# An attention and expert kernel on one core: band tables loaded by SyncE ahead of most value loads, all key tails of the first two batches copied by VectorE, and an instruction order planned with new landing times

## The chip, the core and the metric

The kernel runs on one core of one Trainium2 chip. The metric is the device time of one execution in microseconds (us). A time below is the median of the executions of a kernel, with the number of executions or the range. Profiled executions have a span, which is the profiler's own measure of the same execution and lies 1.7 to 2.4 us below the device time.

Engines are called TensorE (PE in the profile; PEld is its weight load), VectorE (DVE), ScalarE (ACT), GpSimd (POOL) and SyncE (SP, which here only issues DMAs). A ratio is the mean time of one kernel's fast runs over the mean time of the fast runs of the kernel before in the same rounds on the same chip, so it is not quite the ratio of the medians quoted beside it.

## The reference

The reference is attention with a relative position bias, followed by one expert layer with a sine gate. All inputs and the output are float32.

```python
# attention: q, k, v are (8 batches, 8 heads, 576, 64), bias_table is (32, 8)
scores = matmul(q, k^T) / sqrt(64) + bias_table[bucket(|i - j|)]   # bucket is constant for far keys
attn   = exp(scores - max); attn = attn / (sum(attn) + 1e-9)
x      = matmul(attn, v)            # heads put side by side: (8*576, 512) = (4608, 512)
# expert: w_in (512, 2048), w_out (2048, 512), alpha (2048,)
h = x @ w_in
g = h + sin(alpha * h)**2 / (alpha + 1e-9)
out = g @ w_out                     # (4608, 512)
```

The bias of far keys is one constant per head, so only a band near the diagonal needs correcting. The kernel multiplies that band of exp(scores) by exp(bias difference).

## The kernel before

The kernel works batch by batch, two heads (a "pair", `p`) at a time. Score matmuls go into a PSUM tile `sc`; ScalarE writes exp(sc) into a buffer `u`; VectorE multiplies the near-diagonal band of `u` by tables `m2r` and `mhr`; TensorE multiplies `u` by the values (`v`, and `vh` for the last 64 keys); the result is normalized and transposed into `xT`; the expert matmuls `sc<-xT,w_in`, the sine, the square, `g` and the `w_out` matmuls follow. The expert stage of one batch is mixed with the attention of later ones.

Three details matter.

First, the band tables are made on the chip: a small matmul and exp give an 8-row table `e_sb`, which is written to DRAM (`e_dram`, 8 KB) and read back with overlapping rows as `m2r` and `mhr`. These reads must wait for the write.

Second, the last 64 keys of a pair are multiplied from a block-diagonal copy `kts` (`kt` in the profile, the "key tails"). In the kernel before, VectorE makes that copy for pairs 0 and 1 of the first batch, and small DMAs of SyncE make it for all others.

Third, everything after the prologue is ordered by a greedy list scheduler, written in Python and run when the kernel is built. It knows only assumed durations and assumed landing times of the loads. Each engine then executes its instructions in that fixed order, whatever really happens.

```python
T_M2 = (16.8, 20.0)        # m2r: first two heads, rest
T_MH = (18.0, 18.0)        # mhr
T_V = (18.5, 45.0)         # values of batch 0, of batch 1
T_TR1 = (33.0, 37.0)       # keys and queries of batch 1
T_W = 30.0                 # w_in
T_WO = (48.5, 50.5, 52.5, 54.0)
FAR = 1
...
class Plan:
    def run(self, t0):
        free = {e: t0 for e in ("PE", "ACT", "DVE", "POOL", "DMA", "SP")}
        todo = list(self.tasks)
        while todo:                      # pick the task that may start first, by the
            ...                          # assumed times; emit it; advance that engine
```

The prologue, cut to what the change touches (`P_` is GpSimd):

```python
    nc.sync.dma_start(out=id_sb, in_=idm.ap())
    ...
    for c in range(4):                                   # values of batch 0: 6 loads, SyncE
        nc.sync.dma_start(out=vst[0][:, c], in_=vp[128 * c : 128 * c + 128])
    for z in range(2):
        nc.sync.dma_start(out=vhst[0][64 * z : 64 * z + 64], in_=vq[z, 512:S])
    ...
    nc.scalar.activation(out=e_sb, in_=eps_[0:H, 0:EW], func=AF.Copy)
    nc.scalar.dma_start(out=e_dram.ap(), in_=e_sb)       # 8 KB write
    cast0(0, nc.vector)
    cast0(1, P_)
    clear(P_, 1)
    load_m2r(P_, 0, 2)                                   # reads of e_dram, by GpSimd
    load_mhr(P_)
    cast_v(0, P_, (0, 1))                                # values to 16 bit
    load_m2r(P_, 2, H)
    load_w_in16((0,))
    cast_v(0, P_, (2, 3, 4, 5))
    load_w_in16((1, 2, 3))
    for kq, src in ((0, k), (1, q)):
        load_nat(nat2[:, kq], 0, H, src[1], P_)          # keys, queries of batch 1
    load_v32(1, P_)
    load_w_out16()
    cast_v(1, P_, range(6))
```

The key tails:

```python
        far = kq == 0 and (t == 1 or p > FAR)
        ...
        if far:                          # by a DMA of SyncE, for one or two pairs at a time
            ...
            def split(e):
                load_kt(t, p0, p1)
            y = plan.add({"DMA": D_SPLIT}, split, [z[1] for z in ps_], pri)
            ...
            return [x], []

        def tail(e):                     # by VectorE
            for z in range(2):
                r = slice(64 * z, 64 * z + 64)
                nc.vector.tensor_copy(
                    out=kts[t][r, p, r], in_=kTs[t][r, p, 512:S]
                )
```

The softmax here doesn't subtract the row's maximum and nothing guards it: scores larger than these inputs give would overflow.

Of the kernel before, what the change touches and what calls it, by code (L numbers as in the profile page):

```python
# [24 lines left out]
def t_act(n):  # L25
    return n / 1200.0 + 0.052
# [27 lines left out]
class Cell:  # L54
    v = None
# [123 lines left out]
T_MODE = 0.11  # L179
T_START = 7.0  # L180
T_PAIR = ((7.0, 8.5), (10.5, 13.0), (10.5, 13.0))
T_M2 = (16.8, 20.0)
T_MH = (18.0, 18.0)
T_V = (18.5, 45.0)
T_TR1 = (33.0, 37.0)
D_SPLIT = 3.5
T_W = 30.0
# [1 line left out]
WARM0 = 6  # L189
WARM1 = 1  # L190
AV_PRI = 2000
FAR = 1
NORM_PRI = -300
CP_PRI = -1
SIN_SET = "trig_and_small"
# [15 lines left out]
def kernel(  # L211
# [11 lines left out]
    nc = tc.nc  # L223
    T, H, S, D = q.shape
# [48 lines left out]
    vst, vhst = [], []  # L273
# [108 lines left out]
    def load_kt(t, p0, p1):  # L382
        for z in range(2):
            r = slice(64 * z, 64 * z + 64)
            nc.sync.dma_start(out=kts[t % 2][r, p0:p1, r], in_=kTs[t % 2][r, p0:p1, 512:S])
# [16 lines left out]
                out=vhs[t % 2][64 * z : 64 * z + 64, :, VC * z : VC * z + D], in_=vq[z, 512:S]  # L402
            )

    def load_v32(t, eng):
        vp = v[t].rearrange("h s d -> s h d")
        for c in range(4):
            eng.dma_start(out=vst[t][:, c], in_=vp[128 * c : 128 * c + 128])
        vq = v[t].rearrange("(hp two) s d -> two s hp d", two=2)
        for z in range(2):  # L410
            eng.dma_start(out=vhst[t][64 * z : 64 * z + 64], in_=vq[z, 512:S])

    def cast_v(t, eng, cs):
        for c in cs:
            if c < 4:
                eng.tensor_copy(out=vs[t][:, c, :, 0:D], in_=vst[t][:, c])
                continue
            z = c - 4
            eng.tensor_copy(
                out=vhs[t][64 * z : 64 * z + 64, :, VC * z : VC * z + D],  # L420
                in_=vhst[t][64 * z : 64 * z + 64],
            )

    def load_nat(dst, h0, h1, src, eng):

        eng.dma_start(out=dst, in_=src[h0:h1].rearrange("h (p i) d -> p h (i d)", i=SI))
# [35 lines left out]
    def load_m2r(eng, h0, h1):  # L462

        eng.dma_start(
            out=m2r[:, h0:h1],
            in_=bass.AP(tensor=e_dram, offset=EW * h0, ap=[[1, 128], [EW, h1 - h0], [1, XW]]),
        )

    def load_mhr(eng):
        for z in range(2):  # L470
            eng.dma_start(  # L471
                out=mhr[64 * z : 64 * z + 64],
                in_=bass.AP(tensor=e_dram, offset=EW * z + 192,
                            ap=[[1, 64], [2 * EW, NP], [1, 192]]),
            )

    P_ = nc.gpsimd
# [4 lines left out]
        out=tabL,  # L482
        in_=bass.AP(tensor=bias_table.tensor, offset=bias_table.offset + (NB - 1) * H,
                    ap=[[0, NB], [1, H]]),
# [2 lines left out]
    nc.scalar.dma_start(out=alphaN, in_=moe_alpha.rearrange("(f p) -> f p", p=128))  # L487
    nc.scalar.dma_start(out=idf_sb, in_=idf.ap())
    nc.sync.dma_start(out=id_sb, in_=idm.ap())
    nc.scalar.preload_act_table_set(EXP_SET)  # L490
    for kq, src in ((0, k), (1, q)):
        load_nat(nat1[:, kq, 0:2], 2, 4, src[0], P_)
    vp = v[0].rearrange("h s d -> s h d")
    for c in range(4):
        nc.sync.dma_start(out=vst[0][:, c], in_=vp[128 * c : 128 * c + 128])
    vq = v[0].rearrange("(hp two) s d -> two s hp d", two=2)
    for z in range(2):
        nc.sync.dma_start(out=vhst[0][64 * z : 64 * z + 64], in_=vq[z, 512:S])
    for kq, src in ((0, k), (1, q)):
        load_nat(nat1[:, kq, 2:6], 4, H, src[0], P_)  # L500

# [10 lines left out]
    cast0(0, nc.vector)  # L512
    cast0(1, P_)
    clear(P_, 1)
    load_m2r(P_, 0, 2)
    load_mhr(P_)
    cast_v(0, P_, (0, 1))
    load_m2r(P_, 2, H)
    load_w_in16((0,))
    cast_v(0, P_, (2, 3, 4, 5))  # L520
    load_w_in16((1, 2, 3))
    for kq, src in ((0, k), (1, q)):
        load_nat(nat2[:, kq], 0, H, src[1], P_)
# [4 lines left out]
    plan = Plan()  # L528
# [8 lines left out]
        else:  # L537
            k_of(e).tensor_copy(out=o, in_=i)  # L538

    farq, split_of = [], {}  # L540

    def plan_tr(t, p, kq, pri, nb, deps=()):

        b, c = Buf("moE"), Cell()
        far = kq == 0 and (t == 1 or p > FAR)

        def mm(e):
            c.v = bank("moE").bitcast(F16)
            for i in range(SI):
                x = i * SN  # L550
                if t == 0 and p == 0:
                    nc.tensor.transpose(
                        out=c.v[:, x : x + SN], in_=natb[:, kq, i], identity=id_sb[0:SN, 0:SN]
                    )
                    continue
                for z in range(2):
                    h = 2 * p - 2 + z if t == 0 else 2 * p + z
                    nc.tensor.transpose(
                        out=c.v[64 * z : 64 * z + 64, x : x + SN],
                        in_=(nat1 if t == 0 else nat2)[:, kq, h, D * i : D * i + D],  # L560
                        identity=id_sb[0:SN, 0:SN],
                    )

        def cp(e):
            pin = c.v[:, 0:S].rearrange("d (i p) -> d p i", i=SI)

            dst = (qTs if kq else kTs)[t][:, p, :]
            copy_on(e, dst.rearrange("d (p i) -> d p i", i=SI), pin)

        m = plan.add({"PE": 0.4 if t == 0 and p == 0 else 0.5}, mm, deps, pri, nb, new=[b])  # L570
        eng = {"DVE": 0.75, "ACT": 0.72}
        if t == 0:
            eng = {"ACT": 0.72} if p == 0 and kq else {"DVE": eng["DVE"]}
        x = plan.add(eng, cp, [m], pri, use=[b])
        if kq:
            return [x], [x]
        if far:
            farq.append((p, x))
            if t and p % 2 == 0:
                return [x], []  # L580
            ps_ = [y for y in farq]
            farq.clear()
            p0, p1 = ps_[0][0], ps_[-1][0] + 1

            def split(e):
                load_kt(t, p0, p1)

            y = plan.add({"DMA": D_SPLIT}, split, [z[1] for z in ps_], pri)
            for z in ps_:
                split_of[(t, z[0])] = y  # L590
            return [x], []

        def tail(e):
            for z in range(2):
                r = slice(64 * z, 64 * z + 64)
                nc.vector.tensor_copy(
                    out=kts[t][r, p, r], in_=kTs[t][r, p, 512:S]
                )

        return [x], [plan.add({"DVE": 0.25}, tail, [x], pri + 30)]  # L600
# [90 lines left out]
    def plan_ex(t, y, sc, b, u, ub, m, gate, base, done):  # L691

        p, i = y

        def ex(e):
            uz = u.v[:, 0:8, :].rearrange("p (z c) q -> p z c q", z=2)
            if i == "t":
                o = u.v[:, 8, :].rearrange("p (b q) -> p b q", b=2)
                x = sc.v[:, :, 0:288]
            elif i < 4:  # L700
                o, x = uz[:, :, i, 0:512], sc.v
            else:
                o = uz[:, :, :, 512:576]
                x = sc.v[:, :, 0:256].rearrange("p z (c q) -> p z c q", c=4)
            nc.scalar.activation(out=o, in_=x, func=AF.Exp, scale=0.125)  # L705

        n = 576 if i == "t" else 1024 if i < 4 else 512
        x = plan.add({"ACT": t_act(n)}, ex, [m] + gate, base + 20, use=b + [ub])
        if i == "t":

            def bh(e):
                io = u.v[:, 8, 384:576]
                nc.vector.tensor_tensor(out=io, in0=io, in1=mh[:, p, 0:192], op=ALU.mult)

            done[(0, 4)] = x
            done[(1, 4)] = plan.add({"DVE": 0.19}, bh, [x], base + 10,
                                     nb=0.0 if t else T_MH[p > 0], use=[ub])
            return x
        w = 0 if i < 4 else 1
        q0, n = QW[w]  # L720
        for cc in [i] if i < 4 else range(4):
            done[(w, cc)] = x
            lo, hi = max(q0, 128 * cc - 128), min(q0 + n, 128 * cc + 256)
            if lo >= hi:
                continue

            def bd(e, cc=cc, lo=lo, hi=hi):
                io = u.v[:, 0:8, lo:hi].rearrange("p (z c) q -> p z c q", z=2)[:, :, cc]
                x0 = lo - 128 * cc + 128
                nc.vector.tensor_tensor(  # L730
                    out=io, in0=io, in1=m2[:, 2 * p : 2 * p + 2, x0 : x0 + hi - lo],
                    op=ALU.mult,
                )

            done[(w, cc)] = plan.add({"DVE": 0.1 + (hi - lo) / 960.0}, bd, [x], base + 10,
                                     nb=0.0 if t else T_M2[p > 0], use=[ub])
        return x

# [3 lines left out]
    def plan_av(t, p, w, u, ub, done):  # L742
# [14 lines left out]
        for i, qc in enumerate(QC[w]):  # L757

            def mm(e, i=i, qc=qc):
# [5 lines left out]
                for z in range(2):  # L765
                    for c in range(4):
# [4 lines left out]
            prev = [plan.add({"PE": 0.31}, mm, us + prev, base + AV_PRI + i,  # L771
                             nb=T_V[t] if t < 2 else 0.0, new=[ab] if i == 0 else [],
                             use=[ub] if i == 0 else [ub, ab])]
# [266 lines left out]
```

## Time and profile before

| kernel before | |
|---|---|
| time | 392.61 us, median of 3 runs (392.54 to 392.93) |
| span of the profiled execution | 392.2 us |
| TensorE busy | 96% |
| first value matmul of batch 0 | 19.60 us |
| first expert matmul | 35.80 us |
| first score matmul of the third batch | 54.96 us |

The last three are marks from the timeline: the first ends the load phase, the second ends the start, and the third ends the first expert stage. After them comes a steady stretch of some 337 us.

The first fence shows the head of the page of the kernel before: the span, the busy time of each engine with its share and number of instructions, and three of the rows that cut the span into 40 slices of 9.8 us each. In these rows a digit is the busy share in tenths (PE, DMA), or the granted clock of TensorE in tenths (PEclk).

```profile
span 392.2 us, 8566 instructions
...
PE 378.4 (96%) x3401; PEld 190.1 (48%) x3401; DVE 262.0 (67%) x587; ACT 323.9 (83%) x458; POOL 81.9 (21%) x96
...
PE   6989999999999999999999999999999999999995
...
PEclk9989999999999999999999999999999999999999
DMA  9999999999726999991996497211014000020122
```

TensorE is full except in the first slices and the last, and the DMA row reads 9 in each of the first ten slices, 98 us.

The next fence shows the kernel before in four stretches cut at the marks. The columns are start and end, length, busy time of TensorE, its weight load, VectorE, ScalarE and GpSimd with their instructions, then granted clock, DMA share and GB/s. (The DMA share adds up the times of packets over 16 engines; it exceeds 1 here, up to 1.44.)

```profile
0.00:20.00 20.00, 16.16 (x135) 7.24 (x135) 9.84 (x25) 12.12 (x15) 13.00 (x28) 1.00 1.03 191
20.00:36.00 16.00, 13.62 (x234) 9.82 (x233) 12.47 (x44) 12.06 (x15) 8.25 (x12) 0.89 1.13 205
36.00:55.00 19.00, 17.47 (x167) 8.70 (x165) 15.43 (x29) 16.30 (x29) 14.59 (x17) 1.00 1.44 205
55.00:392.00 337.00, 331.18 (x2872) 164.31 (x2871) 224.24 (x492) 283.41 (x401) 46.09 (x40) 1.00 0.83 92
```

The last stretch has TensorE busy for 331 of 337 us. So a change of the first 55 us moves the total one for one, as long as the steady stretch stays as it is.

The chain of waits of the kernel before (start, duration, what) shows how the tables come in:

```profile
7.04 5.33 DMA e_dram<-e_sb
...
12.66 0.73 POOL m2r L464
13.39 1.27 POOL mhr L471 x2
14.66 1.08 POOL v L416 x2
15.74 6.42 DMA m2r<-e_dram
```

The 8 KB write takes 5.33 us; GpSimd then issues the reads with value casts in between, so that the larger part of `m2r` is issued only at 15.74 us and lands at 22.16 us.

Lines of the timeline of the kernel before, in order of time (start, duration, engine, line, operation, in brackets the idle time before and what ended it):

```profile
17.89 0.61 PE L450 MATMUL sc<-qT,kT 64*128 64x512 f16 x2
...
17.94 2.35 DVE L730 TENSOR_TENSOR u<-u,m2r 128x512 f16<-128x512 f16 x4 [2.24 <-DMA m2r<-e_dram]
...
18.24 1.31 POOL L419 CAST vh<-w_out 64x256 f16<-64x256 f32 x2
...
19.60 0.22 PE L450 MATMUL am<-vh,u 128*128 128x130 f16 x1
...
22.18 0.42 DVE L730 TENSOR_TENSOR u<-u,m2r 128x512 f16<-128x512 f16 x1 [1.43 <-DMA m2r<-e_dram]
...
35.80 0.81 PE L450 MATMUL sc<-xT,w_in 128*128 128x512 f16 x3
...
54.96 0.39 PE L450 MATMUL sc<-qT,kT 64*128 64x512 f16 x2 [0.64 <-DVE g L879]
```

VectorE stands idle for 3.7 us in all for the two parts of `m2r`. The last value cast ends at 19.55 us, and the first value matmul starts 0.05 us later. (The value casts read from `w_out`, because the space of `w_out` holds the raw values at the start.)

A warning about the clock: the profile counts full clock until the first change that it recorded, which is at 19.3 us in the kernel before. The matmuls show that this is wrong: the two score matmuls at 17.89 us took 0.61 us and two of the same form at 54.96 us took 0.39 us, so TensorE was not at full clock there, although PEclk reads 9.

### The profile page before, as it was taken

To read this page: it belongs to the slowest core of one execution; us is meant where nothing else is said; L and a number is where in the kernel's file an instruction comes from. 1 tells how busy PE (TensorE), PEld (TensorE's weight loads), DVE (VectorE), ACT (ScalarE), POOL (GpSimd) and SP (SyncE) were. 2 spreads that over 40 slices of the span, in tenths; PEclk is the share of its full clock that TensorE was granted. 3 is DMA by queue.
4 is the path that set the end of the run, shared out by engine and by line. 5 is a ranking of instruction groups with operands and counts; after the bars stand their busy time and mean duration, and the time that the engine had idled before them with its cause. 6 is when DMAs were issued, how large, how long until landed. Compare 5 with 4: busy or idle time off the path is not lost.

```text
span 392.2 us, 8566 instructions
## 1 busy us (share of the span) xinstructions
PE 378.4 (96%) x3401; PEld 190.1 (48%) x3401; DVE 262.0 (67%) x587; ACT 323.9 (83%) x458; POOL 81.9 (21%) x96
## 2 busy tenths in 40 slices
PE   6989999999999999999999999999999999999995
PEld 2456445644455554445445544554445444444442
DVE  3576987768576689567967895768676869429100
ACT  2976999979899999999989999999999969539211
POOL 5762963090004545001700310000000000000000
PEclk9989999999999999999999999999999999999999
DMA  9999999999726999991996497211014000020122
GB/s 170 211 204 219 207 171 158 166 171 148 92 59 83 158 155 157 158 166 47 150 170 101 34 93 166 68 33 42 27 43 59 17 28 29 27 80 2 57 76 80
DMA packets 148647, 41.99 MB, mean 107 GB/s; under 512 B 137784, under 2 KB 142992, under 8 KB 148608
## 3 DMA queue, kind: packets, MB, share of 16 engines
q0 software_dynamic: 89872, 19.04, 56.9%
q1 hardware_dynamic: 58512, 22.36, 30.3%
q8 instruction: 26, 0.43, 0.5%
q14 instruction: 13, 0.11, 0.1%
q10 hardware_dynamic: 224, 0.05, 0.1%
HBM read 37.76 MB, written 16.52 MB: 138 GB/s over the span
## 4 chain that ended last, share of the span: by engine, by line
PE 86%; DMA 4%; DVE 4%; ACT 3%; POOL 1%; issue 1%; ACTq 0%; DVEq 0%
PE sc L450 41%; PE am L450 34%; PE cb L450 5%; PE ca L450 5%; ACT u L705 2%; DMA m2r<-e_dram 2%; DMA e_dram<-e_sb 1%; DMA phi_sb<-phi_const 1%; DVE g L879 1%; DVE u L730 1%; ACT s L865 1%; DVE xn L785 1%; DVE outs L538 0%; DVE kT L538 0%; POOL mhr L471 0%
## 5 line engine op out<-in xcount | busy, mean ns | idle before, releaser
L705 ACT ACTIVATE u<-sc 128x1024 f16<-128x1024 f32 (+1 forms) x192 | 157.8, 898 | 14.4 <-PE sc L450 12.9
L450 PE MATMUL sc<-xT,w_in 128*128 128x512 f16 x576 | 132.3, 379 | 0.6 <-DVE g L879 0.5
L879 DVE SCALAR_TENSOR_TENSOR g<-sq,inv_a,sc 128x512 f16<-128x512 f16 x144 | 103.3, 746 | 22.1 <-PE am L450 14.7
L450 PE MATMUL am<-w_out,g 128*128 128x512 f16 x416 | 108.6, 380 | 0.3 <-DVE outs L538 0.2
L865 ACT ACTIVATE s<-sc,alphaT 128x512 f16<-128x512 f32 x144 | 92.7, 678 | 6.4 <-PE sc L450 5.0
L730 DVE TENSOR_TENSOR u<-u,m2r 128x512 f16<-128x512 f16 (+2 forms) x160 | 67.7, 438 | 32.4 <-ACT u L705 27.8
L450 PEld LDWEIGHTS <-w_in 128*128 128x128 f16 x576 | 55.3, 98 | 65.0 <-issue 1.3
L450 PEld LDWEIGHTS <-g 128*128 128x128 f16 x576 | 53.3, 98 | 64.1 <-issue 11.6
L450 PEld LDWEIGHTS <-u 128*128 128x128 f16 x1440 | 55.8, 98 | 19.2 <-issue 11.0
L450 PE MATMUL sc<-qT,kT 64*128 64x64 f16 (+1 forms) x512 | 50.8, 297 | 1.7 <-ACT u L705 0.9
L450 PE MATMUL am<-v,u 128*128 128x65 f16 x1152 | 51.2, 194 | 0.0
L872 ACT ACTIVATE sq<-s 128x512 f16<-128x512 f16 x79 | 49.2, 628 | 2.2 <-DVE g L879 0.5
L396 POOL DMA_DIRECT2D v<-in_v_dram x24 | 22.2, 1065 | 119.6 <-PE am L450 104.3
L874 DVE TENSOR_TENSOR sq<-s 128x512 f16<-128x512 f16 x65 | 27.4, 423 | 9.2 <-ACT s L865 8.8
L450 PE MATMUL am<-vh,u 128*128 128x130 f16 x144 | 32.2, 224 | 0.8 <-DVE xp L785 0.8
L450 PEld LDWEIGHTS <-kT 64*128 64x128 f16 x512 | 14.7, 96 | 28.5 <-issue 24.3
L785 DVE TENSOR_TENSOR xp<-am,rd 128x384 f16<-128x384 f32 (+1 forms) x48 | 23.6, 491 | 1.8
L784 DVE RECIPROCAL rd<-am 128x6 f32<-128x6 f32 (+1 forms) x56 | 10.5, 187 | 19.7 <-PE am L450 19.2
L450 PE MATMUL cb<-w_out,g 128*128 128x512 f16 x96 | 23.0, 380 | 0.0
L937 ACT ACT_TABLE_LOAD x13 | 16.7, 1283 | 0.2
L377 POOL DMA_DIRECT2D staged_q<-in_q_dram x6 | 15.5, 2583 | 3.6 <-DMA staged_q<-in_q_dram 3.6
L538 DVE COPY outs<-am 128x512 f32<-128x512 f32 x19 | 13.1, 688 | 4.3 <-PE am L450 4.1
(88 smaller groups left out, 175.6 us busy)
## 6 DMA issues: line engine op xcount, KB each, us to landing
out_dram<-outs SPq DMA_DIRECT2D x36, 256.0 KB, 2.2
staged_k<-in_k_dram POOLq DMA_DIRECT2D x6, 576.0 KB, 13.8
staged_q<-in_q_dram POOLq DMA_DIRECT2D x6, 576.0 KB, 19.7
v<-in_v_dram POOLq DMA_DIRECT2D x24, 128.0 KB, 7.0
w_in<-in_moe_w_in_dram POOLq DMA_DIRECT2D x4, 512.0 KB, 8.8
w_out<-in_moe_w_out_dram POOLq DMA_DIRECT2D x4, 512.0 KB, 10.7
w_out<-in_v_dram SPq DMA_DIRECT2D x4, 256.0 KB, 8.2
v1st<-in_v_dram POOLq DMA_DIRECT2D x4, 256.0 KB, 16.6
```

The lines of the kernel that those rows point to most:

```text
L377: nc.gpsimd.dma_start(out=dst.ap()[t].rearrange("s (h d) -> s h d", h=H), in_=src[t].rearrange("h s d -> s h d"),)
L396: nc.gpsimd.dma_start(out=vs[t % 2][:, c, :, 0:D], in_=vp[128 * c : 128 * c + 128],)
L450: nc.tensor.matmul(out=out, lhsT=lhsT, rhs=rhs, start=start, stop=stop)
L538: k_of(e).tensor_copy(out=o, in_=i)
L705: nc.scalar.activation(out=o, in_=x, func=AF.Exp, scale=0.125)
L730: nc.vector.tensor_tensor(out=io, in0=io, in1=m2[:, 2 * p : 2 * p + 2, x0 : x0 + hi - lo], op=ALU.mult,)
L785: nc.vector.tensor_tensor(out=y.rearrange("p c (z d) -> p c z d", z=2), in0=a[:, :, :, 0:D], in1=r.unsqueeze(3).to_broadcast([128, nq, 2, ...
L865: nc.scalar.activation(out=s16.v, in_=h.v, func=AF.Sin, scale=alphaT[:, f : f + 1])
L872: nc.scalar.activation(out=sq.v, in_=s16.v, func=AF.Square)
L874: k_of(e).tensor_tensor(out=sq.v, in0=s16.v, in1=s16.v, op=ALU.mult)
L879: nc.vector.scalar_tensor_tensor(out=gcell[b].v[:, f, :], in0=sq.v, scalar=inv_a[:, f : f + 1], in1=h.v, op0=ALU.mult, op1=ALU.add,)
L937: nc.scalar.preload_act_table_set(name)
```

## The change

The change wants the tables earlier. It lets SyncE issue their reads, and puts four of the six value loads behind them. It makes all key tails of the first two batches by VectorE copies instead of DMAs. And it plans the order with landing times that are thought to fit the new loads.

```diff
-T_M2 = (16.8, 20.0)
-T_MH = (18.0, 18.0)
-T_V = (18.5, 45.0)
+T_M2 = (13.0, 15.5)
+T_MH = (14.0, 14.0)
+T_V = (18.0, 45.0)
...
-FAR = 1
... (load_v32 takes the chunks to load as an argument: cs=range(6))
     nc.sync.dma_start(out=id_sb, in_=idm.ap())
+    load_v32(0, nc.sync, range(2))
...
-    (four loads vst[0], two loads vhst[0], all on nc.sync)
...
-    load_m2r(P_, 0, 2)
-    load_mhr(P_)
-    cast_v(0, P_, (0, 1))
-    load_m2r(P_, 2, H)
+    load_m2r(nc.sync, 0, 2)
+    load_mhr(nc.sync)
+    load_m2r(nc.sync, 2, H)
+    load_v32(0, nc.sync, range(2, 6))
     load_w_in16((0,))
-    cast_v(0, P_, (2, 3, 4, 5))
+    cast_v(0, P_, range(6))
     load_w_in16((1, 2, 3))
...
-        far = kq == 0 and (t == 1 or p > FAR)
... (the branch for far tails is gone: all go by the VectorE copy)
-            done[(w, cc)] = plan.add({"DVE": 0.1 + (hi - lo) / 960.0}, bd, [x], base + 10,
+            done[(w, cc)] = plan.add({"DVE": (0.14 if t else 0.2) + (hi - lo) / 960.0}, bd, [x], base + 10,
                                      nb=0.0 if t else T_M2[p > 0], use=[ub])
```

The last lines change only what the scheduler assumes that a band multiply takes.

More of the change, by code (lines that the diff above doesn't have):

```diff
@@ L403, in load_v16, with load_v32 @@
             )
-    def load_v32(t, eng):
+    def load_v32(t, eng, cs=range(6)):
         vp = v[t].rearrange("h s d -> s h d")
-        for c in range(4):
+        for c in [c for c in cs if c < 4]:
             eng.dma_start(out=vst[t][:, c], in_=vp[128 * c : 128 * c + 128])
         vq = v[t].rearrange("(hp two) s d -> two s hp d", two=2)
-        for z in range(2):
+        for z in [c - 4 for c in cs if c > 3]:
             eng.dma_start(out=vhst[t][64 * z : 64 * z + 64], in_=vq[z, 512:S])
@@ L492 @@
         load_nat(nat1[:, kq, 0:2], 2, 4, src[0], P_)
-    vp = v[0].rearrange("h s d -> s h d")
-    for c in range(4):
-        nc.sync.dma_start(out=vst[0][:, c], in_=vp[128 * c : 128 * c + 128])
-    vq = v[0].rearrange("(hp two) s d -> two s hp d", two=2)
-    for z in range(2):
-        nc.sync.dma_start(out=vhst[0][64 * z : 64 * z + 64], in_=vq[z, 512:S])
     for kq, src in ((0, k), (1, q)):
@@ L538, in copy_on @@
             k_of(e).tensor_copy(out=o, in_=i)
-    farq, split_of = [], {}
+    split_of = {}
     def plan_tr(t, p, kq, pri, nb, deps=()):
         b, c = Buf("moE"), Cell()
-        far = kq == 0 and (t == 1 or p > FAR)
         def mm(e):
@@ L576, in plan_tr @@
             return [x], [x]
-        if far:
-            farq.append((p, x))
-            if t and p % 2 == 0:
-                return [x], []
-            ps_ = [y for y in farq]
-            farq.clear()
-            p0, p1 = ps_[0][0], ps_[-1][0] + 1
-            def split(e):
-                load_kt(t, p0, p1)
-            y = plan.add({"DMA": D_SPLIT}, split, [z[1] for z in ps_], pri)
-            for z in ps_:
-                split_of[(t, z[0])] = y
-            return [x], []
         def tail(e):
```

## The prediction

> **What bounds it now.** TensorE is 96% busy (engine table), and nearly full in the table by stretches from 36 us on: 40.06 of 41 us, then 39.5 to 39.9 of 40. Slack is in the first 36 us and the last 3. The change pays almost only if the first expert matmul (35.8 us) and first sine (39.1 us) come earlier.
>
> **First 36 us.** The chain of waits runs: bucket matmul, e_sb, the 8 KB write of e_dram (7.04 us, 5.33 us to land at 12.4), GpSimd's m2r issues, the rest of m2r (issued 15.74, 6.42 us, landed 22.2). In the timeline VectorE waits for m2r at 17.94 (2.24 us) and 22.18 (1.43 us). The first attention-value matmul starts at 19.60, just after GpSimd's last value cast ends (19.55). ScalarE's exps run 9.83 to 33.53: 20.7 us busy, 3.0 us idle in six gaps (up to 1.16 us at 28.29, score matmuls queueing behind late value matmuls). TensorE drops to half clock (0.65 us for eight 65-column matmuls instead of 0.40) from about 26.1 to 29.5.
>
> **What the change does.**
> - Only two of six value loads stand before the e_dram write. m2r leaves from SyncE: the first two heads land near 14 us (was 17.9), the rest near 16.5 to 17.5 (was 22.2).[...]
> - Removed: eight key-tail DMAs, landing in about 5 us but never last on the chain. Added: twelve 64x64 VectorE copies at about 0.18 us (0.36 us per pair now), some 1.4 us of them in the first expert stage, where VectorE has slack (about 80% busy).
> - Later loads: four value loads (640 KB) land after m2r, w_in's first quarter earlier. DMA is saturated (about 200 GB/s), but its dip at 14 to 18 us gets filled. I expect the last value cast at 19 to 20 us, no real gain.
> - The order moves on all engines throughout; work per engine stays nearly the same.
>
> **On the critical path.** Bands no longer hold the second pair's value matmuls (25.4 us now; about 22.5 then), an exp buffer comes free in time, and ScalarE runs almost gapless: 9.83 + 20.7 + about 0.8 = 31.3 us instead of 33.5. The tail (2.3 us) stays. So about 2.2 us of start; I take 0.2 off for added VectorE work, reordering and w_out. Estimate: 392.6 - 2.0 = 390.6 us, range 389.0 to 392.2. Faster by over 2%: 0.02; within 2%: 0.97; slower: 0.01.
>
> **What shows it.** Right: VectorE waits for m2r at most 1 us in total (3.7 now); exps end near 31 us, first expert matmul near 33.5, first sine near 37; every later stage is shifted by the same 2 us with TensorE still 99% full. e_dram lands by 11.5. Wrong: the first value matmul waits for value casts until 21 us or later. Score matmuls stand behind it in TensorE's order, ScalarE idles, and the gain is gone. Or VectorE, whose band multiplies now precede the last pairs' query copies, holds these back while m2r is late.
>
> **What would make it wrong.** Late values (above; w_in's first quarter now competes); the clock dropping again in the start; w_out landing (about 54 us now) after its earlier use, about 52; the new order costing or gaining a microsecond in the steady stages.

The landings near 14 us and near 16.5 to 17.5 us are estimates.

## The result, and the profile after

The kernel after took 403.63 us (median of 4 runs, 402.63 to 404.15) against 392.77 us for the kernel before (4 runs, 392.54 to 394.08). The ratio is 1.0267, with a 95% interval of 1.0235 to 1.0298: slower by over 2%. All outputs were correct.

The head of the page after has the same rows; a slice is now 10.06 us.

```profile
span 402.4 us, 8557 instructions
...
PE 379.9 (94%) x3399; PEld 190.8 (47%) x3399; DVE 269.9 (67%) x601; ACT 323.0 (80%) x456; POOL 78.8 (20%) x92
...
PE   5758969999999999999999999999999999999996
...
PEclk8559969999999999999999999999999999999999
DMA  9959999979911999999999196230013100010122
```

Nearly the same work is done in 10.2 us more. The loss lies in the first seven slices: PE reads 5758969 there where it read 6989999, the clock shows 5, 5 and 6 in three of them (its first change was recorded at 4.5 us here and at 19.3 us before, so the first two slices of the clock cannot be compared), and the third slice of the DMA row has fallen from 9 to 5. VectorE is busy for 7.9 us longer with only 14 instructions more.

The kernel after, cut at the same marks, which now fall at 24.27, 40.04 and 65.25 us:

```profile
0.00:24.00 24.00, 13.92 (x121) 6.23 (x122) 13.11 (x36) 12.17 (x15) 9.12 (x23) 0.66 0.89 178
24.00:40.00 16.00, 14.53 (x240) 10.40 (x240) 10.50 (x36) 11.98 (x15) 8.89 (x13) 0.86 1.02 182
40.00:65.00 25.00, 20.79 (x174) 9.53 (x170) 20.69 (x36) 16.34 (x29) 17.13 (x19) 0.86 1.69 189
65.00:402.00 337.00, 330.68 (x2872) 164.60 (x2870) 225.58 (x496) 282.56 (x398) 43.62 (x39) 1.00 0.80 89
```

| mark | before, us | after, us | lost up to here |
|---|---|---|---|
| first value matmul of batch 0 | 19.60 | 24.27 | 4.7 |
| first expert matmul | 35.80 | 40.04 | 4.2 |
| first score matmul of the third batch | 54.96 | 65.25 | 10.3 |
| end of the span | 392.2 | 402.4 | 10.2 |

So the start lost 4.2 us, the first expert stage lost 6.0 us more, and the last 337 us lost nothing.

**The start.** The waits of SyncE's queue in the kernel after, on its line that reads `e_dram` (in total, times, longest), and then its chain of waits:

```profile
SPq L463 <- DMA e_dram<-e_sb: 6.2, 1, 6.2
```

```profile
6.98 5.12 DMA e_dram<-e_sb
...
12.12 0.37 SPq L463
...
15.07 1.57 SPq L407
...
16.69 5.81 DMA w_out<-in_v_dram
...
23.80 0.42 POOL vh L418
```

SyncE waited 6.2 us for the write to land at 12.1 us. Only then did it issue the tables (L463 is `m2r`), and behind them, from 15.07 us on, the four value loads (L407). One of these took 5.81 us and landed at 22.50 us; the casts followed; the first value matmul started at 24.27 us. The write itself took 5.12 us instead of 5.33 us, although only two value loads instead of six were ahead of it. The wait of 6.2 us is on SyncE's line, and it holds back loads that need no `e_dram` at all.

**The first expert stage.** Timeline lines of the kernel after:

```profile
15.86 1.70 DVE L707 TENSOR_TENSOR u<-u,m2r 128x512 f16<-128x512 f16 x4 [2.29 <-DMA m2r<-e_dram]
...
20.71 0.90 DVE L707 TENSOR_TENSOR u<-u,m2r 128x512 f16<-128x512 f16 x2 [1.72 <-DMA m2r<-e_dram]
...
24.27 0.27 PE L449 MATMUL am<-vh,u 128*128 128x130 f16 x1 [4.16 <-POOL vh L418]
...
25.89 0.60 ACT L682 ACTIVATE u<-sc 128x512 f16<-128x512 f32 x1 [5.09 <-PE sc L449]
...
48.30 2.20 POOL L376 DMA_DIRECT2D staged_k<-in_k_dram  x1
...
49.22 3.71 DVE L573 COPY kt<-kT 64x64 f16<-64x64 f16 x2
...
50.00 2.72 POOL L376 DMA_DIRECT2D staged_q<-in_q_dram  x1
...
52.95 1.41 DVE L856 SCALAR_TENSOR_TENSOR g<-sq,inv_a,sc 128x512 f16<-128x512 f16 x2
...
53.75 6.23 PE L449 MATMUL sc<-xT,w_in 128*128 128x512 f16 x16 [3.35 <-DVE g L856]
```

The tables did land earlier: VectorE could start on the two parts at 15.86 and 20.71 us instead of 17.94 and 22.18 us. But the values came later, TensorE waited 4.16 us for the last cast, and score matmuls that stand behind the value matmul in TensorE's order left ScalarE idle for 5.09 us.

At 49.22 us two 64x64 copies of key tails take 3.71 us. One of them alone took 3.51 us, where the median of its kind is below 0.2 us. It ended at 52.73 us, when GpSimd's issue of the `staged_q` load ended (50.00 + 2.72). The next `g` had to wait for VectorE, TensorE idled for 3.35 us, and its next 16 matmuls took 6.23 us where 16 of the same kind take 3.45 us in later stages, since the granted clock was at one half from 52.3 to 59.1 us. That is 3.35 + 2.8 us, about the 6.0 us that the stage lost.

### The profile page after: what moved, and what is told of

The parts are those of the page before. It is cut to its first block, busy times and chain, and to the rows that moved or that the text cites. A ratio compares the mean times of both kernels' runs of the same rounds, so it can differ in the third digit from the quotient of the medians.

```text
span 402.4 us, 8557 instructions
## 1 busy us (share of the span) xinstructions
PE 379.9 (94%) x3399; PEld 190.8 (47%) x3399; DVE 269.9 (67%) x601; ACT 323.0 (80%) x456; POOL 78.8 (20%) x92
## 4 chain that ended last, share of the span: by engine, by line
PE 86%; DVE 4%; DMA 4%; ACT 3%; SPq 1%; issue 1%; POOL 0%; ACTq 0%
PE sc L449 41%; PE am L449 34%; PE cb L449 5%; PE ca L449 4%; ACT u L682 2%; DMA w_out<-in_v_dram 1%; DMA e_dram<-e_sb 1%; DMA phi_sb<-phi_const 1%; DVE g L856 1%; DVE kt L573 1%; DVE xp L762 1%; SPq L407 0%; SPq L470 0%; DVE sq L851 0%; SPq L463 0%
## 5 line engine op out<-in xcount | busy, mean ns | idle before, releaser
L449 PE MATMUL sc<-xT,w_in 128*128 128x512 f16 x576 | 134.4, 385 | 4.2 <-DVE g L856 4.2
L449 PE MATMUL am<-w_out,g 128*128 128x512 f16 x416 | 110.3, 380 | 1.0 <-ACT outs L530 0.7
L842 ACT ACTIVATE s<-sc,alphaT 128x512 f16<-128x512 f32 x144 | 92.1, 679 | 12.5 <-PE sc L449 12.1
L849 ACT ACTIVATE sq<-s 128x512 f16<-128x512 f16 x77 | 47.9, 629 | 2.4 <-DVE g L856 0.5
L532 DVE COPY outs<-am 128x512 f32<-128x512 f32 x21 | 14.5, 688 | 8.0 <-PE am L449 8.0
L376 POOL DMA_DIRECT2D staged_q<-in_q_dram x6 | 15.5, 2586 | 1.5 <-DMA staged_q<-in_q_dram 1.5
## 6 DMA issues: line engine op xcount, KB each, us to landing
v1st<-in_v_dram POOLq DMA_DIRECT2D x4, 256.0 KB, 15.8
```

The lines of the kernel that those rows point to most:

```text
L376: nc.gpsimd.dma_start(out=dst.ap()[t].rearrange("s (h d) -> s h d", h=H), in_=src[t].rearrange("h s d -> s h d"),)
L449: nc.tensor.matmul(out=out, lhsT=lhsT, rhs=rhs, start=start, stop=stop)
L532: k_of(e).tensor_copy(out=o, in_=i)
L842: nc.scalar.activation(out=s16.v, in_=h.v, func=AF.Sin, scale=alphaT[:, f : f + 1])
L849: nc.scalar.activation(out=sq.v, in_=s16.v, func=AF.Square)
```

## The experiments

The theory after this reading has three parts. **T (tails):** a plain 16-bit copy on VectorE that meets GpSimd's DMA instructions is held until they end. **L (loads):** the four late value loads inherit SyncE's wait for `e_dram`. **O (order):** the instruction order was planned with landing times that did not come true, and it costs time by itself. Rivals are: the copies cost through the new order and not by being held; the values are late because `w_in` takes the bandwidth; and the half clock at the start causes the loss. Fifteen kernels ran. All were correct. Medians of the kernel before lay at 392.69, 393.07, 393.12 and 392.72 us in the four sets of rounds.

| run | time, us | ratio | first value matmul | first expert matmul | third batch's scores |
|---|---|---|---|---|---|
| before | 392.77 | 1 | 19.60 | 35.80 | 54.96 |
| after | 403.63 | 1.0267 | 24.27 | 40.04 | 65.25 |
| e1_tails_dma | 398.86 | 1.0158 | 24.15 | 39.65 | 59.05 |
| e2_tails_tt | 399.61 | 1.0183 | 24.38 | 40.10 | 60.31 |
| e8_before_dve_tails | 398.53 | 1.0148 | 21.25 | 35.52 | 61.60 |
| e3_v_pool | 399.80 | 1.0176 | 23.43 | 40.08 | 60.50 |
| e4_v_pool_tt | 398.19 | 1.0143 | 23.67 | 39.97 | 60.01 |
| e5_w_in_late | 404.56 | 1.0296 | 23.35 | 38.80 | 65.19 |
| e16_before_new_times | 396.75 | 1.0105 | 23.16 | 38.17 | 57.22 |
| e17_new_loads_old_times | 398.05 | 1.0137 | 24.01 | 38.79 | 59.57 |
| e10_true_times | 401.81 | 1.0227 | 25.30 | 44.04 | 63.32 |
| e13_true_nat | 396.63 | 1.0092 | 25.23 | 36.77 | 58.13 |
| e15_before_measured | 395.14 | 1.0052 | 21.12 | 38.41 | 58.03 |
| e11_v_first_w_late | 393.77 | 1.0020 | 19.16 | (32.14) | 53.77 |
| e14_v_first_measured | 396.16 | 1.0070 | 23.45 | 38.56 | 57.28 |
| e12_v_pool_tt_w_late | 395.94 | 1.0074 | 20.36 | 36.29 | 56.69 |
| e18_before_tables_sp | 392.14 | 0.9990 | | | |

The medians of e4 and e18 are those of their three fast runs. The profile of e18 is not used, as told there. In e11 the plan put two expert matmuls ahead of the rest of the start, so that its mark is not comparable; its first sine is used instead. The marks come from one profiled execution each. That of the kernel before had a stretch at half clock (26.1 to 29.5 us) and a device time of 393.95 us, some 1.2 us above its other runs, so differences of spans and of times need not agree within a microsecond.

### Tails

**e1_tails_dma** is the kernel after with the second batch's tails made by DMA again, as before (the first batch's stay copies).

```diff
+        far = kq == 0 and t == 1
... (the branch `if far:` as in the kernel before)
```

> Changed kernel, but the second batch's key tails go by DMA again. Theory A (two separate losses: late values cost about 4.2 us of start, a 3.5 us VectorE tail copy plus the clock drop behind it cost about 6 us in the first expert stage): about 397.5 us, no copy over 1 us in the first expert stage, first expert matmul still near 40 us. Rival (the 10 us are all one loss, the late start, which disturbs everything planned after it): about 403 us, and the first expert stage stays 6 us longer than before whatever does the tails.

It took 398.86 us instead of 403.63 us. The first expert stage shrank from 25.2 us (65.25 - 40.04) to 19.4 us (59.05 - 39.65), which is what it takes in the kernel before (19.2 us). The start stayed as late. So the tails are worth 4.8 us of the loss, and loads and order the rest, 6.2 us (398.86 - 392.69).

**e2_tails_tt** keeps the copies in the same place in VectorE's order, but writes them as a two-input operation, the maximum of the tail with itself.

```diff
-                nc.vector.tensor_copy(
-                    out=kts[t][r, p, r], in_=kTs[t][r, p, 512:S]
-                )
+                src = kTs[t][r, p, 512:S]
+                nc.vector.tensor_tensor(out=kts[t][r, p, r], in0=src, in1=src, op=ALU.max)
```

> Changed kernel, same order on every engine; each tail copy is written as a two-input maximum of the tail with itself, so same bytes, same place, same engine. Theory A[...]: tails 0.15 to 0.3 us each, no stall, about 397.5 us. Rival 1 (VectorE was late for another reason at that place, such as late data, or the SBUF was busy with DMA writes): the first operation at that place takes 3 us again, about 403 us.

It took 399.61 us. The view of the tile `kt` gives the copies of the second batch's tails with shortest, median and longest duration in ns; first of the kernel after, then of this run, then this run's timeline at the place in question:

```profile
L573 DVE COPY kt<-kT x8: 177/194/3514, 49.2 to 56.9; 64x64 f16<-64x64 f16 x8
```

```profile
L574 DVE TENSOR_TENSOR kt<-kT x8: 175/186/190, 49.3 to 53.0; 64x64 f16<-64x64 f16 x8
```

```profile
48.35 2.20 POOL L376 DMA_DIRECT2D staged_k<-in_k_dram  x1
...
49.26 0.38 DVE L574 TENSOR_TENSOR kt<-kT 64x64 f16<-64x64 f16 x2
...
50.06 2.72 POOL L376 DMA_DIRECT2D staged_q<-in_q_dram  x1
```

GpSimd issued the same two loads at the same time, within 0.06 us, and the same two tails took 0.38 us instead of 3.71 us. The order was the same and the data was the same; only the kind of instruction differed. This excludes the rival that the new order costs the time. Why the one kind is held and the other is not is not shown: the traces give the durations, 3.51 us against 0.19 us, and no mechanism. The two-input form is not always short either: in e13 below, two tails in that form ran beside GpSimd's value casts and took 0.59 and 0.55 us.

**e8_before_dve_tails** does this part of the change alone: the kernel before with all tails copied by VectorE.

```diff
-        far = kq == 0 and (t == 1 or p > FAR)
+        far = False
```

> The kernel before with all key tails as VectorE copies, loads and landing times as before: this part of the change alone. [...]the first second-batch tail stands behind GpSimd's [...]staging of k and q (44.6 to 49.1 us in the kernel before) and takes 3 to 4 us, ending with it[...]: 396 to 399 us. Rival (the copies cost only their 0.18 us, and the loss came with the late start): 392.5 to 393.5 us.

It took 398.53 us, 5.5 us more than the kernel before (393.07 us in these rounds). Its start was as early as before (first expert matmul at 35.52 us) and the first expert stage took 26.1 us. Its timeline:

```profile
46.55 2.22 POOL L377 DMA_DIRECT2D staged_k<-in_k_dram  x1
...
47.19 4.87 DVE L596 COPY kt<-kT 64x64 f16<-64x64 f16 x4
...
48.27 2.71 POOL L377 DMA_DIRECT2D staged_q<-in_q_dram  x1
...
52.89 3.45 PE L450 MATMUL sc<-xT,w_in 128*128 128x512 f16 x8 [4.33 <-DVE g L879]
```

Again the copy that met these two GpSimd instructions took 3.80 us and ended with the second of them (48.27 + 2.71 = 50.98 us). TensorE waited 4.33 us for `g`, then ran at half clock until 56.0 us: eight matmuls took 3.45 us, as long as 16 take at full clock. Two copies at 14.51 us took 2.45 us as well, beside GpSimd's table loads and casts. So this part needs nothing else of the change to cost over 5 us.

The instruction records of the four runs with plain copies (after, e8, and e3 and e5 below) show this in more detail. Eleven second-batch tail copies that ran beside GpSimd's DMA instructions took 0.21 to 3.80 us instead of 0.18, and each of them ended within 0.005 us of the end of one of these instructions. Others ran in 0.18 us just after such an end, while the next instruction was already on record; so a copy is held until a running instruction ends (the second of two in the longest cases), not during the whole series.

The clock fell in both kernels while TensorE waited for `g`, but not after the same time: in e8 about 4.1 us after the last matmul (48.56 to 52.6 us), in the kernel after 1.9 us after it (50.41 to 52.3 us). In the kernel before it fell at 26.1 us without a long stall: TensorE had been busy for 4.37 us of the stretch from 20 to 26 us, and none of its idle stretches there lasted over 1.0 us. What makes the clock fall is not shown by these runs.

### Loads

**e3_v_pool** moves the four late value loads from SyncE to GpSimd, which does not wait for `e_dram` any more.

```diff
     clear(P_, 1)
+    load_v32(0, P_, range(2, 6))
     load_m2r(nc.sync, 0, 2)
     load_mhr(nc.sync)
     load_m2r(nc.sync, 2, H)
-    load_v32(0, nc.sync, range(2, 6))
     load_w_in16((0,))
```

> Changed kernel, but the four late value loads are issued by GpSimd at about 8 us instead of by SyncE behind the e_dram wait. Theory A (values are late since SyncE issues them only after e_dram has landed at 12.1 us and the tables have been issued): last value cast before 18.5 us, first value matmul at 18 to 19.5 us, first expert matmul near 35 us, about 398.5 us, the copy stall still there. Rival (values are late because the DMA engines have no bandwidth left, with w_in's first quarter added): last cast still after 21 us, time 401.5 to 403 us.

It took 399.8 us. The values came in time: the last cast ended at 16.4 us instead of 24.2 us. Yet the first expert matmul stood at 40.08 us, not earlier at all. The tables now came late instead: `m2r` landed at 19.85 and 24.77 us (15.9 and 20.7 in the kernel after), and TensorE waited 4.6 us for a query copy, which stands behind band multiplies in VectorE's order. The 3.8 us of total time that it gained over the kernel after has another source: GpSimd's two staged loads were over at 46.2 us, so the tail copies met only its shorter value loads.

```profile
L573 DVE COPY kt<-kT x8: 166/178/632, 49.1 to 53.2; 64x64 f16<-64x64 f16 x8
```

The longest copy took 0.63 us. This supports T from another side, and it is a failure of L alone: removing SyncE's wait for the values moved the wait and did not remove it.

**e4_v_pool_tt** is e3 with the two-input tails of e2 (both edits above).

> Both mendings together: values issued by GpSimd and tails as two-input maximum. Theory A, losses add: about 392 us (391 to 393.5), that is about 11 us under the changed kernel and near the kernel before. If the band tables really help (my prediction's mechanism), 390.5 to 391.5.

It took 398.19 us (median of three; the fourth run, 405.08 us, was slow and is not counted). The gains are not additive, and my expectation of about 392 us failed. Its timeline shows where the start went:

```profile
20.09 1.70 DVE L706 TENSOR_TENSOR u<-u,m2r 128x512 f16<-128x512 f16 x4 [5.19 <-DMA m2r<-e_dram]
...
22.81 0.59 PE L449 MATMUL cb<-zz 128*128 128x512 f16 x1 [3.59 <-DVE qT L532]
```

The first part of `m2r`, 192 KB, was issued at 12.31 us and landed only at 20.09 us: with the value loads in flight on another queue it took 7.8 us, where it took 3.6 us in the kernel after. VectorE idled 5.19 us in front of it, and the query copy for the next pair stood behind it.

**e5_w_in_late** tests the rival that the first quarter of `w_in` takes the bandwidth: in the kernel after, that load moves behind the casts.

```diff
-    load_w_in16((0,))
     cast_v(0, P_, range(6))
-    load_w_in16((1, 2, 3))
+    load_w_in16((0, 1, 2, 3))
```

> The changed kernel with w_in's first quarter issued after the first batch's value casts, as nothing but the order of GpSimd's loads. Issue theory (values late because SyncE waits for e_dram until 12.1 us): e_dram within 0.7 us of 12.1, values land at most 1.5 us earlier, last cast 22.5 to 24 us, 401.5 to 404 us. Bandwidth theory: tables land 2 us and values 3 us or more earlier, first value matmul by 21 us, 399 to 400.5 us.

It took 404.56 us. The tables landed 0.6 and 0.9 us earlier (15.25 and 19.79 us), the last cast ended at 23.3 us instead of 24.2 us. So bandwidth is about 0.9 us of the lateness of the values, and the rival falls for the other 3.8 us. The start became 1.2 us shorter, but the first expert stage grew to 26.4 us: the tail copies met GpSimd's loads again, four of them took 4.52 us.

The third rival, half clock at the start, is not settled by this run: PEclk reads 9 there in e5 and e3, but their first recorded change is at 26.5 and 27.7 us, and eight 65-column matmuls took 0.65 us at 23.4 us in e5, where they take 0.40 us at full clock. What speaks against it is where the time went. From the first value matmul to the first expert matmul, the kernel before took 16.2 us with 3.4 us of half clock on record, and the kernel after 15.8 us with 4.1 us. So what delays the start lies before the first value matmul, where TensorE stood waiting (4.16 us for the last cast in the kernel after). No run varied the clock alone.

### Order

The next two runs complete a square. One puts the change's landing times alone into the kernel before; the other keeps the new loads but plans with the old times. Both have the second batch's tails by DMA, so T does not enter.

**e16_before_new_times:**

```diff
-T_M2 = (16.8, 20.0)
-T_MH = (18.0, 18.0)
-T_V = (18.5, 45.0)
+T_M2 = (13.0, 15.5)
+T_MH = (14.0, 14.0)
+T_V = (18.0, 45.0)
```

> Kernel before, loads and tails untouched, the order planned with the change's landing times (13.0, 15.5, 14.0, 18.0). If the order is what loses: band multiplies stand before the last query copies while the tables land at 17.9 and 22.2 us, first expert matmul at 37.5 to 39 us, 394.5 to 396.5 us. If the late loads alone lose it: within 0.7 us of the kernel before.

**e17_new_loads_old_times** is e1 with the three old constants (the same diff, reversed).

> Changed kernel's loads, second-batch tails by DMA, order planned with the landing times of the kernel before (16.8, 20.0, 18.0, 18.5). Values still land near 23 us and are planned for 18.5, so the first value matmul still stands in front of score matmuls: if the values decide, first expert matmul 38.5 to 40 us and 397 to 399 us; if the tables' planned times decided, 36 to 37.5 us and 394 to 396 us.

| first expert matmul, time | old landing times | new landing times |
|---|---|---|
| old loads | 35.80 us, 392.7 us (before) | 38.17 us, 396.75 us (e16) |
| new loads | 38.79 us, 398.05 us (e17) | 39.65 us, 398.86 us (e1) |

Five numbers in the plan, with every load as it was, cost 4.0 us. The new loads with the old plan cost 5.3 us. Both together cost 6.2 us. (Two small differences remain in the square: the new loads' row has the first batch's far tails as copies and the changed assumed cost of a band multiply.) What TensorE waited for, in e16 and then in e17 (in total, times, longest):

```profile
PE cb L450 <- DVE qT L538: 3.8, 1, 3.8
```

```profile
PE am L449 <- POOL vh L418: 3.9, 1, 3.9
```

In e16 the plan believes in tables at 13 us, so it puts band multiplies ahead of query copies on VectorE. The tables land when they always did, VectorE stands idle for 4.29 us in front of the first band multiply until 17.75 us (the profile's view of waits puts this down to ScalarE's exp, but by the semaphore records VectorE's wait for `m2r` ended at 17.69 us, 0.03 us after the landing), and TensorE waits 3.8 us for the queries. In e17 the order is good for the old loads, but the values come late and TensorE waits 3.9 us for their cast. Each half breaks the start by a different wait. With both (e1) the waits are not added up: TensorE waited 1.1 us for a query copy and then 3.4 us for the values.

**e10_true_times** starts from e2 and plans with the landings measured in the trace of the kernel after.

```diff
-T_M2 = (13.0, 15.5)
-T_MH = (14.0, 14.0)
-T_V = (18.0, 45.0)
+T_M2 = (15.9, 20.7)
+T_MH = (17.9, 17.9)
+T_V = (24.2, 45.0)
```

> The two-input tails, and the order planned with the landing times that the changed kernel's trace shows (tables 15.9 and 20.7 us, 17.9 for the tail table, value casts 24.2) in place of 13.0, 15.5, 14.0 and 18.0. Loads are the changed kernel's. Theory B (the start is lost since TensorE and VectorE are ordered for landings that do not come: late value matmuls stand before score matmuls, late band multiplies before query copies): exps run almost gapless from 9.6 to 31 or 32 us although tables and values land just as late, first expert matmul 34 to 36 us, about 392.5 us (391 to 394). Rival (the late landings themselves cost the start, whatever the order): first expert matmul still near 40 us, about 398.5 us or more.

It took 401.81 us, worse than e2 (399.61 us). The exps were nearly without a gap, from 10.26 to 33.13 us. But a landing that I had not corrected broke the order elsewhere:

```profile
38.94 0.69 PE L551 MATMUL am<-id_sb,nat 96*64 96x96 f16 x12 [5.13 <-DMA nat<-in_k_dram]
```

The plan expected the second batch's keys at 33 us. They landed at 38.9 us, because all of GpSimd's later loads stand behind the casts, and their transposes had been put ahead of the last value matmuls. TensorE stood for 5.13 us.

**e13_true_nat** corrects this time as well.

```diff
-T_TR1 = (33.0, 37.0)
+T_TR1 = (39.0, 42.0)
```

> As the run with the measured landing times, and also the second batch's k and q planned for 39 and 42 us, where they land, in place of 33 and 37. Theory B (the start was lost by an order made for landings that do not come; in the last run its gain was eaten by one more such wait, 5.1 us for k at 33.8 us): no wait of TensorE over 1 us in the start, first expert matmul near 35 to 36 us, first sine 38 to 40 us, 392.5 to 395.5 us (w_in and w_out land some 3 us later than before and may cost 1 to 2 us). Rival: still over 398 us.

It took 396.63 us, 3.0 us less than e2. The first expert matmul came at 36.77 us instead of 40.10 us, although the first value matmul came no earlier (25.23 us); part of this was given back in the next stage, so that the third batch's scores came 2.2 us earlier. So about half of what loads and order cost together can be had back by the order alone, with loads as late as they are.

**e15_before_measured** asks whether measured landings are always better: the kernel before, planned with its own measured landings.

```diff
-T_M2 = (16.8, 20.0)
+T_M2 = (17.9, 22.2)
-T_V = (18.5, 45.0)
+T_V = (19.6, 45.0)
```

> The kernel before, its order planned with the landings its own trace shows (17.9, 22.2, 18.0, 19.6 us in place of 16.8, 20.0, 18.0, 18.5), nothing else. If planning with landings 1 to 2 us too early costs it anything: 390.5 to 392 us. If not: within 0.5 us of the kernel before.

They are not. It took 395.14 us, 0.5% more than the kernel before, and the first expert matmul came at 38.41 us. TensorE waited 1.7 us for the second batch's keys. The plan is greedy, and its old constants had been tuned with that order: an estimate that is right in one place moves other items to places where their own estimates are wrong.

### A better version?

**e11_v_first_w_late** has SyncE issue all six value loads first and the tables after them, all of `w_in` after the casts, the second batch's tails by DMA, and landing times set between.

```diff
-T_M2 = (13.0, 15.5)
-T_MH = (14.0, 14.0)
-T_V = (18.0, 45.0)
+T_M2 = (16.0, 19.0)
+T_MH = (17.0, 17.0)
+T_V = (17.0, 45.0)
...
-    load_v32(0, nc.sync, range(2))
+    load_v32(0, nc.sync)
...
-    load_v32(0, nc.sync, range(2, 6))
-    load_w_in16((0,))
     cast_v(0, P_, range(6))
-    load_w_in16((1, 2, 3))
+    load_w_in16((0, 1, 2, 3))
... (tails as in e1)
```

> Candidate: all six value loads first on SyncE as before, then the tables on SyncE, w_in behind the casts, second-batch tails by DMA, order planned with 16.0, 19.0, 17.0 (tail table) and 17.0 (values). Expected landings: tables near 16 and 19.5, last cast near 16.5 us; first value matmul 18 to 19 us, first expert matmul near 34 us, 390.5 to 392 us, about 1 us below the kernel before. If the tables land after 20 us, 393 to 396.

It took 393.77 us, ratio 1.0020. With no load behind the wait for `e_dram`, the casts ended at 17.0 us, the first value matmul came at 19.16 us and the first expert sine at 37.59 us instead of 39.09 us. The third batch's scores started 1.2 us before those of the kernel before, but the total is the same (interval 1.0002 to 1.0039).

**e14_v_first_measured** is e11 planned with e11's measured landings (`T_M2` 18.7 and 21.2, `T_MH` 20.0, `T_V` 17.1).

> Candidate: the version with all values first, planned once more with its own measured landing times (18.7, 21.2, 20.0, 17.1). 391.5 to 394 us; below 392 only if the start gains another 0.5 to 1 us.

It took 396.16 us. The first value matmul moved to 23.45 us: having planned for a later table, the order itself made the value matmul later. It is e15's result a second time.

**e12_v_pool_tt_w_late** is e4 with all of `w_in` after the casts (the edit of e5).

> Values issued by GpSimd at about 8 us and two-input tails, with w_in's first quarter behind the value casts. If the tables were late there (20.1 us) since other loads stood before them on the DMA engines, they land at 17 to 18 us now, the query copy that waits behind the band multiplies is on time, first expert matmul 36 to 38 us, 394 to 396.5 us. If the tables stay after 19.5 us: near 398 us again.

It took 395.94 us, 2.3 us less than e4. The tables landed at 16.74 and 20.16 us instead of 20.09 us and later. So bandwidth matters where value loads and tables are in flight together, although it hardly did in e5.

**e18_before_tables_sp** is the kernel before with one idea of the change: tables read by SyncE behind all six value loads, `w_in` behind the casts, tails as before.

```diff
-T_M2 = (16.8, 20.0)
+T_M2 = (17.0, 19.8)
-T_V = (18.5, 45.0)
+T_V = (17.5, 45.0)
...
-    load_m2r(P_, 0, 2)
-    load_mhr(P_)
-    cast_v(0, P_, (0, 1))
-    load_m2r(P_, 2, H)
-    load_w_in16((0,))
-    cast_v(0, P_, (2, 3, 4, 5))
-    load_w_in16((1, 2, 3))
+    load_m2r(nc.sync, 0, 2)
+    load_mhr(nc.sync)
+    load_m2r(nc.sync, 2, H)
+    cast_v(0, P_, range(6))
+    load_w_in16((0, 1, 2, 3))
```

> Candidate: kernel before, all six value loads first on SyncE, then the tables on SyncE, w_in behind the casts, planned with 17.0, 19.8, 18.0, 17.5; tails as before. Tables near 18 and 21 us, casts done near 17 us: 391 to 393.5 us, at best 1 us under the kernel before.

Its three fast runs took 391.05, 392.14 and 393.21 us, ratio 0.9990 with an interval of 0.9961 to 1.0019: the same. Its profiled execution was the fourth, which fell into a slow state (541.88 us at a granted clock of 0.663), so its profile is not used. No version that ran beats the kernel before clearly.

## Why the prediction was wrong

The prediction said 390.6 us (389.0 to 392.2) and gave 0.01 to slower by over 2%. The kernel took 403.63 us. These steps of it failed.

- **"I expect the last value cast at 19 to 20 us, no real gain."** It ended at 24.2 us. The step counted the bytes (640 KB behind the tables) and not the place: the four loads stand on SyncE behind the reads of `e_dram`, and SyncE waited 6.2 us for the write. They were issued only from 15.07 us on. It was not bytes that the casts waited for: the DMA share fell from 9 tenths to 5 in the slice from 20 to 30 us, since GpSimd's next loads stood behind those casts (issued from 24.16 us on). e11 and e3, where no value load is behind that wait, had their casts done at 17.0 and 16.4 us.
- **"e_dram lands by 11.5"; first tables "near 14 us", the rest "near 16.5 to 17.5".** The write landed at 12.1 us; it took 5.12 us with two value loads ahead of it, and 5.33 us with six. The tables landed at 15.9 and 20.7 us. The waits of VectorE for `m2r`, predicted at "at most 1 us in total", were 4.0 us (3.7 before).
- **The trust in the plan.** The estimate of "ScalarE runs almost gapless" took the new landing constants (13.0, 15.5, 14.0 and 18.0 us) as harmless. e16 shows that these constants alone, with the loads untouched, cost 4.0 us. The prediction did name the mechanism among what would show it wrong, namely band multiplies that hold back query copies, but gave it no weight in the number: TensorE waited 1.2 us for that in the kernel after, 3.8 us in e16 and 3.6 us in e4.
- **"twelve 64x64 VectorE copies at about 0.18 us ... where VectorE has slack"; "I take 0.2 off for added VectorE work".** Most copies did take about 0.18 us. One took 3.51 us, and the half clock that followed nearly doubled the price. e1 against the kernel after puts this at 4.8 us, and e8 alone at 5.5 us. The duration was read from copies that met no DMA instruction of GpSimd; the prediction did not ask what GpSimd does at the new place.

What was right: the change moves the first 55 us only, the steady stretch took 337 us in both kernels, and it is the first expert matmul that tells the start. The first of the listed ways to be wrong ("The first value matmul waits for value casts until 21 us or later. Score matmuls stand behind it in TensorE's order, ScalarE idles") is what happened: 24.27 us, and 5.09 us of idle ScalarE. It was seen and given too small a chance. What did not follow is the estimate that fewer loads ahead would let the write land by 11.5 us: with two value loads ahead of it instead of six it took 5.12 us instead of 5.33 us, 0.2 us less.

Accounted for: about 10.9 us of loss, of which 6.2 us are loads and order (e1 against before) and 4.8 us are tails (after against e1). What stays open: why a plan with measured landings was worse in e15 and e14 is argued from the order and shown only by the waits named there. How the 6 us of the expert stage split into idle time and clock is read from one profile, not separated by a run. And what held the copy is not shown; the runs show only that it ended with GpSimd's DMA instructions (at 52.73 us in the kernel after, 50.98 us in e8) and that a two-input instruction did not wait for them (0.19 us). How much the half clock at the start adds is not shown by a run.

## What to carry to other kernels

A load that stands behind a waiting DMA on the same issuing engine inherits the whole wait (6.2 us here): cost a moved load by when its engine can issue it, not by its bytes, and keep loads that need nothing ahead of those that wait. An order planned with assumed landing times is tuned together with its loads, so changing either without the other cost 4 to 5 us here, and even measured times have to be run before they are believed. Before moving a small copy to VectorE, look at what GpSimd issues at that moment: here a plain 16-bit copy of 64x64 was held until its DMA instructions ended (up to 3.80 us instead of 0.18 us), and a two-input form of it was not (0.19 us; beside GpSimd's casts it took 0.55 and 0.59 us). Count the half clock after a stall too: with it, TensorE's stall of 3.35 us cost about 1.8 times its length, and that of 4.33 us in e8 about 1.4 times. And read the clock from the durations of matmuls where no change of it is on record yet.
